# Fetching the first weight tile ahead of attention, taking weight signs from other words, and splitting the block loads between two queues

## Chip, cores and metric

The kernel runs on one core of one Trainium2 chip. The metric is the device time of one execution in microseconds. The change is judged by the median of several executions of the kernel before and after it.

## What is computed

A retention layer feeds two feed-forward layers. For each of 16 (batch, head) pairs, 768 steps:

```python
state = gamma * state + outer(k[t], v[t])
y[t]  = scale * (q[t] @ state)
x  = y laid out as (1536 tokens, 512)
x  = softplus(x @ w_in) @ w_out                        # m = 0, d_ff = 2048
h  = x @ w2_in
out = (h * clip(h + 3, 0, 6) / 6) @ w2_out              # m = 1
```

The four weight matrices come as 64-bit floats, and are made 32-bit floats on the chip.

## The kernel before

**Attention.** Tokens are taken in 12 units of 128 (two batches of six). Units 0 to 3 (`START`) run first, alone: k and q of a unit are loaded, turned on TensorE by transposes (`ident,k` and `ident,q`), copied out (`kT` by ScalarE, `qT` by VectorE), and give scores (`qT,kT`), masked by VectorE (`pw`), the product with the state (`qT,st`), the new state (`vs,k`) and the inner product (`pw,vs`). The result is split into `x_hi` (ScalarE) and `x_lo` (VectorE), the two parts of x that the GEMM uses. Units 4 to 7 run the same steps between the GEMM's blocks. Units 8 to 11 (`FIRST` and later) have no transposes on TensorE: `blocks` (L446) loads k and q in 16 small DMAs each, of 16 KB in pieces of 128 bytes, into tiles `kb` and `qb`, both halves of the buffer `raw_0`, and VectorE transposes them in 32x32 blocks into `cv` tiles (`in_blocks`). Both have one buffer, so a unit's loads wait until the unit before has been transposed.

**GEMM.** Each matrix is cut into 16 tiles of 256 KB (32-bit); tokens into three chunks of 512. A block of G1 is h = x @ w_in for one tile f (12 matmuls of 512 columns: hi x hi, hi x lo, lo x hi for four parts of the contraction), a block of G2 adds g @ w_out to four accumulating banks, two tiles later (`LAG`). Blocks alternate, G1 and G2, over m, chunk and f: 2304 matmuls of 512 columns, 192 blocks. At the end of a chunk the four accumulating banks are evacuated as the next `x_hi` and `x_lo`.

**Weights.** `weight` (L266) makes one tile: `fetch` (L283, SP, 512 KB of 64-bit words into `raw`), `bits` (ScalarE, the low word's top bits into `cv`), the sign, the high word scaled and clamped, `merge` (VectorE, shift and or), then the high part `w[:, 0]` (ScalarE, `high`) and the low part, either by VectorE (`low`) or by GpSimd as an accumulating DMA (`add`, L323). `sign` (L294) writes the top half of each `cv` word as a 16-bit float, reading the top 16 bits of the high word. For odd tiles of m = 0 and all of m = 1 (`SCALED`) ScalarE scales the high word (`scale`) and VectorE clamps it (`clamp`, one pass); for the others VectorE does both in two passes (`scaled`, `capped`). There are five raw buffers in the first stage, three later, and four `cv` buffers. Tiles of m = 0 are all made in the first pass over f, tiles of m = 1 while m = 0's last chunk and m = 1's first run.

**Order.** The order on each engine is set while the program is built. `Plan` (L25) holds tasks with an engine, a cost, a due time, what they follow and which buffers they take; `run` simulates the engines and emits tasks in the order in which that simulation starts them. Costs and due times so only set the order; on the chip each engine runs its queue in order and waits by semaphores. Every emitted operation has line 44 in the profile, and tiles tell them apart. DMAs are issued by SP (`nc.sync`), the accumulating ones by GpSimd (`nc.gpsimd`); a DMA on SP reuses one of eight semaphores and waits until the DMA eight before it has landed. The due time of the first tile's fetch is set on L329 (`begin + 15`, behind unit 0's and 1's loads).

```python
for e in range(2):                                            # blocks, L450
    r = slice((2 * g + e) * 32, (2 * g + e + 1) * 32)
    for p in range(NP):
        nc.sync.dma_start(out=tile_of(n)[r, p].rearrange("t (x d) -> t x d", x=4), in_=src[g, e, :, p])
```

```python
when -= EDGE * (u < START and eng in ("DVE", "ACT"))          # task, L429
```

Of the kernel before, what the change touches and what calls it, by code (L numbers as in the profile page):

```python
# [10 lines left out]
F32 = mybir.dt.float32  # L11
F32R = mybir.dt.float32r
U32 = mybir.dt.uint32
U16 = mybir.dt.uint16
F16 = mybir.dt.float16
AF = mybir.ActivationFunctionType
ALU = mybir.AluOpType
PSUM = bass.MemoryType.PSUM
P = 128
# [106 lines left out]

PSX, TT, TS, ACP, ACS = 0.61, 0.62, 0.36, 0.49, 0.55
GEMM = 2.73


@with_exitstack
def kernel(ctx, tc, q, k, v, w1_in, w1_out, w2_in, w2_out, table, out):
# [17 lines left out]
    MORE = 2  # L150
    AHEAD = 3
    HOLD = 8.0
    EDGE = 3.0

    def BY_DVE(n):
        return n < 6 or n < 2 * NF and n % 4 != 0

    def SCALED(n):
        return n >= 2 * NF or n % 2 == 1

    tc.nc.scalar.preload_act_table_set("softplus")

# [59 lines left out]
    half = fixed.tile([P, 1], F32, name="half")  # L222
    three = fixed.tile([P, 1], F32, name="three")
    nc.vector.memset(half, -0.5 + 7.5 * 2.0 ** -12)
    edge = fixed.tile([P, 1], F32, name="edge")
    nc.vector.memset(three, 3.0)
    nc.vector.memset(edge, 32767.5 * 2.0 ** -60)


    G = [(m, c, f) for m in range(2) for c in range(NC) for f in range(NF)]  # L230
# [35 lines left out]
    def weight(m, o, f, number):  # L266
        key = m, o, f
        made = conv[0] if m == 0 else []
        use = due[("G2" if o else "G1"), min(m * NC * NF + f, len(G) - LAG)] - 4.0

        def raw():
            return at_slot((f"raw{m}", key))

        def low_word():
            return raw()[:, :, 0]

        def y():
            return raw()[:, :, 1]

        def w():  # L280
            return at_slot((f"cv{m}", key))

        def fetch():  # L283
            src = words[m][o]
            if o:
                nc.sync.dma_start(out=raw().rearrange("p n t -> p (n t)"), in_=src[f * P:(f + 1) * P, :])
            else:
                nc.sync.dma_start(out=raw().rearrange("p (k n) t -> p k (n t)", k=KD),
                                  in_=src[:, 2 * f * P:2 * (f + 1) * P].rearrange("(k p) f -> p k f", p=P))

        def bits():
            nc.scalar.activation(w(), low_word(), AF.Relu, scale=2.0 ** -29 * (1 - 2.0 ** -12), bias=half)

        def sign():  # L294
            top = raw().bitcast(U16)[:, :, 3]
            to = w().bitcast(F16).rearrange("p (n x) -> p n x", x=2)[:, :, 1]
            nc.scalar.activation(to, top, AF.Identity, scale=-2.0 ** -60, bias=edge)

        def scale():
            nc.scalar.activation(y().bitcast(F32), y().bitcast(F32), AF.Copy, scale=2.0 ** -112)  # L300

        def clamp():
            nc.vector.tensor_scalar(y().bitcast(F32), y().bitcast(F32), -TOP, TOP, ALU.max, ALU.min)

        def scaled():
            nc.vector.tensor_scalar(y().bitcast(F32), y().bitcast(F32), 2.0 ** -112, -TOP, ALU.mult, ALU.max)

        def capped():
            nc.vector.tensor_scalar(y().bitcast(F32), y().bitcast(F32), TOP, None, ALU.min)

        def merge():
            nc.vector.scalar_tensor_tensor(w(), y(), 3, w(), ALU.logical_shift_left, ALU.bitwise_or)

        def high():
            nc.scalar.activation(w_part(key, 0), w().bitcast(F32), AF.Copy)

        def negative():
            nc.scalar.activation(w_part(key, 1), w().bitcast(F32), AF.Copy, scale=-1.0)

        def low():  # L320
            nc.vector.tensor_tensor(w_part(key, 1), w().bitcast(F32), w_part(key, 0).bitcast(F32), ALU.subtract)

        def add():  # L323
            nc.gpsimd.dma_start(out=w_part(key, 1).bitcast(F32), in_=w().bitcast(F32), accum_op=ALU.add)

        raw_k, cv_k = (f"raw{m}", key), (f"cv{m}", key)
        cv, part = [(f"cv{m}", cv_k)], [("w", ("w", key))]
        tail = 1.5 if BY_DVE(number) else 7.0
        T["F", key] = t0 = nc.add("SP", 0.45, fetch, due=begin + 15 if number < 1 else use - tail - 8.0, take=[(f"raw{m}", raw_k)], load=1.45 if o else 1.75)  # L329
        t1 = nc.add("ACT", 0.65, bits, [t0], use - tail - 3.5, take=cv)  # L330
        t2 = nc.add("ACT", 0.57, sign, [t1], use - tail - 2.9)
        if SCALED(number):
            t3 = nc.add("ACT", 0.57, scale, [t2], use - tail - 2.3)
            t4 = nc.add("DVE", TS, clamp, [t3], use - tail - 1.9)
        else:
            t3 = nc.add("DVE", TS, scaled, [t2], use - tail - 2.3)
            t4 = nc.add("DVE", TS, capped, [t3], use - tail - 1.9)
        t5 = nc.add("DVE", TT, merge, [t4, t2], use - tail - 1.3, give=[raw_k])
        if BY_DVE(number):
            a = nc.add("ACT", ACS, high, [t5], use - 1.5, take=part, give=[cv_k] + made)  # L340
            b = nc.add("DVE", TT, low, [a], use - 0.7, give=[cv_k] + made)
        else:
            n = nc.add("ACT", ACS, negative, [t5], use - tail, take=part)
            b = nc.add("POOL", 0.9, add, [n], use - tail + 1, give=[cv_k] + made, load=1.6)
            a = nc.add("ACT", ACS, high, [n], use - 2.5, give=[cv_k] + made)
        T["W", key] = [a, b]
# [42 lines left out]
        nc.tensor.transpose(idle[:, i % NP, :], ident, ident)  # L389

    arena = [("arena", j) for j in range(LATE)]

    part = [slice(j * HALF, (j + 1) * HALF) for j in range(2)]

# [26 lines left out]
    def attend(u):  # L421
# [6 lines left out]
        def task(eng, cost, fn, after, when, take=(), give=(), load=0.0, hold=0.0):  # L428
            when -= EDGE * (u < START and eng in ("DVE", "ACT"))  # L429
            return nc.add(eng, cost, fn, after, when, [(p, k) for p, k in take], list(give) + mine, load, hold)  # L430

        def tile_of(n):
            return at_slot((n, u))

        def own(n):
            return [(f"{n}{ph}", (n, u))]
# [9 lines left out]
        def blocks(n):  # L446
            def go():
                src = {"qb": q, "kb": k}[n][b, :, i * C:(i + 1) * C, :].rearrange("(p g) (x t) (e d) -> g e t p x d", g=2, x=4, e=2)
                for g in range(2):
                    for e in range(2):  # L450
                        r = slice((2 * g + e) * 32, (2 * g + e + 1) * 32)
                        for p in range(NP):
                            nc.sync.dma_start(out=tile_of(n)[r, p].rearrange("t (x d) -> t x d", x=4), in_=src[g, e, :, p])
            return go

        def load(n, when, parts=1):
# [5 lines left out]
            at = [d["S" if ph else "Tk"] - 9.0 + x / 2 for x in range(3)]  # L462
        ik, iv = load("k", at[0], 2 if u == 0 else 1), load("v", at[2])
        if ph:
            ikb, iqb = (task("SP", 7.2, blocks(n), [], d["S"] - 25.0, take=own(n), load=2.0, hold=HOLD + d["S"] - 30.0) for n in ("kb", "qb"))
        else:
            iq = load("q", at[1])
        if u == START - 1:
# [34 lines left out]
        if whole:  # L503
# [12 lines left out]
            def masked(g):  # L516
                return lambda: nc.vector.tensor_tensor(at_slot(("pw", u))[:, g], bank(sc[g]),
                                                       full.rearrange("p (n t) -> p n t", n=1).to_broadcast([P, NP, C]), ALU.mult)
# [264 lines left out]
```

## Time and profile before

| | |
|---|---|
| median of 3 runs | 594.3 us (594.19 to 595.33) |
| the profiled execution, its own time | 594.75 us |
| its span | 593.0 us |
| TensorE matmul busy | 580.7 us (98%) |
| ScalarE (ACT) busy | 338.9 us (57%) |
| VectorE (DVE) busy | 302.0 us (51%) |
| GpSimd (POOL) busy | 34.4 us (6%) |

PE is TensorE's matmuls and PEld its weight loads. A busy share is a mean over stages; what one engine's work costs is read from the waits of the engine that sets the end in that stage. Time lines give the start of an instruction, its length, and in brackets the idle time of its engine before it with what ended it. [...] The trace names a buffer after the tile that first had it, so unit 8 to 11's loads appear as `raw`, and their transposed blocks as `cv`.

### The profile page before, as it was taken

What the parts mean: (1) busy time and instruction counts of PE and PEld (TensorE: products, weight loads), DVE (VectorE), ACT (ScalarE), POOL (GpSimd) and SP (SyncE); (2) the same over time, 40 slices, a digit from 0 to 9 for tenths busy, and PEclk for the clock granted to TensorE, in tenths of its full rate; (3) what the DMA queues carried; (4) which work ended last, traced back from release to release, by engine and by line L of the source; (5) the groups of instructions that cost most, each with busy time, mean ns of one, the idle gap of its engine ahead of it and who ended that gap; (6) DMA issues with size and microseconds to landing.
All of it is one profiled execution on the core that took longest, in us unless ns stands there. A gap on an engine that the chain in (4) does not pass through costs nothing.

```text
span 593.0 us, 9082 instructions
## 1 busy us (share of the span) xinstructions
PE 580.7 (98%) x3607; PEld 474.1 (80%) x3607; DVE 302.0 (51%) x531; ACT 338.9 (57%) x552; POOL 34.4 (6%) x46
## 2 busy tenths in 40 slices
PE   8999999999999899999999999999999999999997
PEld 7777877788777688888888788878888888888886
DVE  5998998776556333554555654452412222422223
ACT  3599999974323133788999999962212222222220
POOL 0000010000000000011111122210000000000000
PEclk9999999999999899999999999999999999999999
DMA  9998587513323410156567678720100000100001
GB/s 199 247 269 218 168 209 224 142 19 65 65 33 65 114 38 0 31 131 159 148 147 184 161 198 212 180 50 1 72 0 1 0 1 0 72 0 1 1 1 71
DMA packets 80763, 57.76 MB, mean 97 GB/s; under 512 B 53712, under 2 KB 70352, under 8 KB 80720
## 3 DMA queue, kind: packets, MB, share of 16 engines
q1 hardware_dynamic: 75248, 47.21, 29.1%
q0 software_dynamic: 5472, 9.96, 9.9%
q8 instruction: 28, 0.46, 0.3%
q14 instruction: 15, 0.12, 0.1%
HBM read 44.05 MB, written 3.15 MB: 80 GB/s over the span
## 4 chain that ended last, share of the span: by engine, by line
PE 52%; issue 18%; ACT 18%; DVE 4%; POOL 3%; SPq 3%; DMA 2%; POOLq 0%; DVEq 0%; ACTq 0%
PE banks L44 52%; ACT cv L44 8%; ACT w L44 4%; POOL w L44 3%; SPq L44 3%; ACT raw L44 2%; ACT e L44 1%; ACT hi L44 1%; DVE cv L44 1%; ACT g L44 1%; DMA w<-cv 1%; DVE raw L44 1%; DMA raw<-in_v_dram 1%; DVE g L44 0%; DMA out_dram<-e 0%
## 5 line engine op out<-in xcount | busy, mean ns | idle before, releaser
L44 PE MATMUL banks<-x_hi,w 128*128 128x512 f32 x768 | 253.6, 392 | 0.8 <-ACT w L44 0.3
L44 PEld LDWEIGHTS banks<-x_hi,w 128*128 128x128 f32 x768 | 144.0, 188 | 33.0 <-DVE g L44 1.1
L44 PE MATMUL banks<-x_lo,w 128*128 128x512 f32 x384 | 149.1, 389 | 0.0
L44 PE MATMUL banks<-hi,w 128*128 128x512 f32 x384 | 128.7, 397 | 0.0
L44 PE MATMUL banks<-w,hi 128*128 128x512 f32 (+1 forms) x386 | 118.5, 389 | 1.1 <-DVE x_lo L44 1.1
L44 ACT ACTIVATE e<-banks,three 128x512 f32<-128x512 f32 x48 | 32.8, 684 | 114.5 <-PE banks L44 107.1
L44 DVE TENSOR_TENSOR lo<-g,hi 128x512 fp32r<-128x512 f32 x96 | 66.2, 690 | 53.7 <-ACT hi L44 53.7
L44 DVE SCALAR_TENSOR_TENSOR g<-e,banks 128x512 f32<-128x512 f32 x48 | 33.1, 689 | 113.7 <-ACT e L44 113.4
L44 PEld LDWEIGHTS banks<-hi,w 128*128 128x128 f32 x384 | 72.8, 190 | 16.4 <-ACT hi L44 0.8
L44 PEld LDWEIGHTS banks<-w,hi 128*128 128x128 f32 x386 | 72.2, 188 | 16.7 <-DVE x_lo L44 1.9
L44 ACT ACTIVATE hi<-g 128x512 fp32r<-128x512 f32 x96 | 60.1, 626 | 43.9 <-DVE g L44 41.3
L44 PEld LDWEIGHTS banks<-x_lo,w 128*128 128x128 f32 x384 | 72.1, 188 | 14.6
L44 PE MATMUL banks<-lo,w 128*128 128x512 f32 x192 | 75.9, 395 | 0.5 <-DVE lo L44 0.5
L44 PE MATMUL banks<-w,lo 128*128 128x512 f32 (+1 forms) x193 | 74.9, 388 | 0.0
L44 ACT ACTIVATE w<-cv 128x512 fp32r<-128x512 f32 x102 | 61.2, 622 | 3.8 <-DVE cv L44 3.5
L44 ACT ACTIVATE cv<-raw,edge 128x512 f16<-128x512 uint16 x64 | 55.9, 880 | 1.4
L44 ACT ACTIVATE g<-banks 128x512 f32<-128x512 f32 x48 | 28.1, 586 | 45.9 <-PE banks L44 45.8
L44 POOL DMA_DIRECT2D w<-cv x38 | 33.4, 878 | 358.0 <-ACT w L44 346.7
L44 DVE TENSOR_SCALAR raw<-raw 128x512 f32<-128x512 f32 x80 | 33.9, 427 | 37.4 <-ACT raw L44 33.1
L44 ACT ACTIVATE cv<-raw,half 128x512 uint32<-128x512 uint32 x64 | 48.1, 756 | 1.7 <-DMA raw<-in_moe_w_out_dram 1.1
L44 DVE SCALAR_TENSOR_TENSOR cv<-raw,cv 128x512 uint32<-128x512 uint32 x64 | 43.9, 689 | 1.3
L44 PEld LDWEIGHTS banks<-lo,w 128*128 128x128 f32 x192 | 36.4, 189 | 8.7 <-DVE lo L44 1.5
(59 smaller groups left out, 359.7 us busy)
## 6 DMA issues: line engine op xcount, KB each, us to landing
raw<-in_moe_w_in_dram SPq DMA_DIRECT2D x32, 512.0 KB, 4.1
raw<-in_moe_w_out_dram SPq DMA_DIRECT2D x32, 512.0 KB, 3.7
w<-cv POOLq DMA_DIRECT2D x38, 256.0 KB, 4.1
out_dram<-e SPq DMA_DIRECT2D x11, 256.0 KB, 2.0
q<-in_q_dram SPq DMA_DIRECT2D x8, 256.0 KB, 5.4
v<-in_v_dram SPq DMA_DIRECT2D x8, 256.0 KB, 5.9
k<-in_k_dram SPq DMA_DIRECT2D x7, 256.0 KB, 5.6
raw<-in_k_dram SPq DMA_DIRECT2D x64, 16.0 KB, 1.8
```

Source lines behind the costliest of these rows:

```text
L44: return self.plan.tc.keep_in_program_order(getattr(self.engine, op)(*args, **kwargs))
```

## The change

The fetch of the first tile gets a due time ahead of every attention load. `EDGE`, by which the due times of VectorE's and ScalarE's work for units 0 to 3 are brought forward, goes from 3 to 6. For m = 0 the high word is scaled and clamped by VectorE in two passes for every tile; the sign is written by ScalarE from 32-bit words, for odd tiles from the raw integer ahead of these passes, for even tiles from the clamped word behind them. For m = 1 the scale stays on ScalarE and the sign is taken out of it: VectorE puts it in by a second merge (`masked`, and with 0x80000000, or). Of the 16 small loads of a unit's k, four go to GpSimd, of q eight.

```diff
+SIGN = 0.75
...
-    EDGE = 3.0
+    EDGE = 6.0
...
-    def SCALED(n):
-        return n >= 2 * NF or n % 2 == 1
+    def DIRECT(n):
+        return n % 2 == 1
...
-    edge = fixed.tile([P, 1], F32, name="edge")
     nc.vector.memset(three, 3.0)
-    nc.vector.memset(edge, 32767.5 * 2.0 ** -60)
...
+        def to():
+            return w().bitcast(F16).rearrange("p (n x) -> p n x", x=2)[:, :, 1]
+
         def sign():
-            top = raw().bitcast(U16)[:, :, 3]
-            to = w().bitcast(F16).rearrange("p (n x) -> p n x", x=2)[:, :, 1]
-            nc.scalar.activation(to, top, AF.Identity, scale=-2.0 ** -60, bias=edge)
+            nc.scalar.activation(to(), y().bitcast(I32), AF.Copy, scale=2.0 ** -100)
+
+        def late_sign():
+            nc.scalar.activation(to(), y().bitcast(F32), AF.Copy)
+
+        def masked():
+            nc.vector.scalar_tensor_tensor(w(), y(), 0x80000000, w(), ALU.bitwise_and, ALU.bitwise_or)
...
-        T["F", key] = t0 = nc.add("SP", 0.45, fetch, due=begin + 15 if number < 1 else use - tail - 8.0, take=[(f"raw{m}", raw_k)], load=1.45 if o else 1.75)
+        T["F", key] = t0 = nc.add("SP", 0.45, fetch, due=begin - 2 if number < 1 else use - tail - 8.0, take=[(f"raw{m}", raw_k)], load=1.45 if o else 1.75)
         t1 = nc.add("ACT", 0.65, bits, [t0], use - tail - 3.5, take=cv)
-        t2 = nc.add("ACT", 0.57, sign, [t1], use - tail - 2.9)
-        if SCALED(number):
-            t3 = nc.add("ACT", 0.57, scale, [t2], use - tail - 2.3)
-            t4 = nc.add("DVE", TS, clamp, [t3], use - tail - 1.9)
+        if m:
+            t2 = nc.add("ACT", 0.57, scale, [t0], use - tail - 3.0)
+            t3 = nc.add("DVE", TS, clamp, [t2], use - tail - 2.5)
+            t4 = nc.add("DVE", TT, masked, [t3, t1], use - tail - 2.0)
         else:
-            t3 = nc.add("DVE", TS, scaled, [t2], use - tail - 2.3)
-            t4 = nc.add("DVE", TS, capped, [t3], use - tail - 1.9)
-        t5 = nc.add("DVE", TT, merge, [t4, t2], use - tail - 1.3, give=[raw_k])
+            t2 = nc.add("ACT", SIGN, sign, [t1], use - tail - 2.9) if DIRECT(number) else None
+            t3 = nc.add("DVE", TS, scaled, [t0, t2], use - tail - 2.7)
+            t3 = nc.add("DVE", TS, capped, [t3], use - tail - 2.3)
+            t4 = t2 or nc.add("ACT", SIGN, late_sign, [t1, t3], use - tail - 1.9)
+        t5 = nc.add("DVE", TT, merge, [t3, t4], use - tail - 1.3, give=[raw_k])
...
+    SHARE = {"kb": 2, "qb": 1}
...
-                            nc.sync.dma_start(out=tile_of(n)[r, p].rearrange("t (x d) -> t x d", x=4), in_=src[g, e, :, p])
+                            (nc.gpsimd if p > SHARE[n] else nc.sync).dma_start(out=tile_of(n)[r, p].rearrange("t (x d) -> t x d", x=4), in_=src[g, e, :, p])
...
-            ikb, iqb = (task("SP", 7.2, blocks(n), [], d["S"] - 25.0, take=own(n), load=2.0, hold=HOLD + d["S"] - 30.0) for n in ("kb", "qb"))
+            ikb, iqb = (task("SP", 0.48 * 4 * (SHARE[n] + 1), blocks(n), [], d["S"] - 25.0, take=own(n), load=2.0, hold=HOLD + d["S"] - 30.0) for n in ("kb", "qb"))
```

What the planner makes of it, at three places. In these rows a name is an engine's own list of operations, without times.

SP at the start, before: the tables, then attention's loads (`k_0`, `q_0`, `v_0` are unit 0's first, and unit 4's when they come again), and weight tiles in `raw`.

```order
L44 DMA small<-in_tables_dram 128x20
L44 DMA k_0_121<-in_k_dram 128x4x64 x2
...
L44 DMA v_1_125<-in_v_dram 128x8x64
L44 DMA raw_0_69<-in_moe_w_in_dram 128x4x256
L44 DMA k_2_123<-in_k_dram 128x8x64
...
L44 DMA k_0_121<-in_k_dram 128x8x64
L44 DMA q_0_118<-in_q_dram 128x8x64
L44 DMA v_0_124<-in_v_dram 128x8x64
L44 DMA raw_3_72<-in_moe_w_out_dram 128x1024
```

And SP at the start with the change:

```order
L44 DMA raw_0_69<-in_moe_w_in_dram 128x4x256
L44 DMA small<-in_tables_dram 128x20
L44 DMA k_0_119<-in_k_dram 128x4x64 x2
...
L44 DMA v_1_123<-in_v_dram 128x8x64
L44 DMA k_2_121<-in_k_dram 128x8x64
...
L44 DMA k_0_119<-in_k_dram 128x8x64
L44 DMA raw_3_72<-in_moe_w_out_dram 128x1024
L44 DMA q_0_116<-in_q_dram 128x8x64
L44 DMA v_0_122<-in_v_dram 128x8x64
```

The first tile has gone from the ninth place to the first, and a w_out tile now stands ahead of unit 4's q and v.

TensorE at units 1 and 2, before (`vs_1` is unit 1's, `k_2` and `q_2` unit 2's):

```order
L44 MATMUL banks<-vs_1_131,k_1_122 64x64 x8
L44 MATMUL banks<-ident,k_2_123 128x128 x4
L44 MATMUL banks<-pw_135,vs_1_131 64x128 x8
L44 MATMUL banks<-ident,q_2_120 128x128 x4
L44 MATMUL banks<-qT_0_128,kT_0_127 128x128 x8
```

And with the change:

```order
L44 MATMUL banks<-vs_1_129,k_1_120 64x64 x8
L44 MATMUL banks<-ident,k_2_121 128x128 x4
L44 MATMUL banks<-ident,q_2_118 128x128 x4
L44 MATMUL banks<-pw_133,vs_1_129 64x128 x8
L44 MATMUL banks<-qT_0_126,kT_0_125 128x128 x8
```

Unit 2's q is turned ahead of unit 1's inner product now, so that product stands between it and the scores that need it. Up to the first GEMM matmul that is all that moved on TensorE.

GpSimd with the change, from the last accumulating copy of m = 0 (`w_1311`) to the first of m = 1 (`w_78`); before, these two kinds of copies follow each other with nothing between:

```order
L44 DMA w_1311<-cv_1_75 128x512
L44 DMA raw_0_69<-in_k_dram 32x4x32 x4
L44 DMA raw_0_69<-in_q_dram 32x4x32 x8
L44 DMA raw_0_69<-in_k_dram 32x4x32 x4
L44 DMA raw_0_69<-in_q_dram 32x4x32 x8
L44 DMA raw_0_69<-in_k_dram 32x4x32 x4
L44 DMA raw_0_69<-in_q_dram 32x4x32 x8
L44 DMA raw_0_69<-in_k_dram 32x4x32 x4
L44 DMA raw_0_69<-in_q_dram 32x4x32 x8
L44 DMA w_78<-cv_0_74 128x512
```

Twelve loads of each of the units 8 to 11 have come to GpSimd, and all stand ahead of m = 1's copies. On TensorE the scores of units 8 to 11 moved with them: they stood behind 38, 42, 47 and 51 blocks of the GEMM, and stand behind 36, 39, 44 and 50.

## Rows read from the trace of the kernel before

**Rows 1.** The page, part 1: busy us, share of the span, instructions.
```profile
PE 580.7 (98%) x3607; PEld 474.1 (80%) x3607; DVE 302.0 (51%) x531; ACT 338.9 (57%) x552; POOL 34.4 (6%) x46
```

**Rows 2.** Windows: stretch, its length; busy us (instructions) by engine; clock; DMA share; GB/s.
```profile
core 0: us, PE busy (x) PEld busy (x) DVE busy (x) ACT busy (x) POOL busy (x), PEclk, DMA share, GB/s
27.11:113.56 86.45, 85.56 (x804) 67.55 (x805) 77.39 (x150) 84.28 (x141) 4.88 (x6) 1.00 0.78 213
...
200.00:320.00 120.00, 120.00 (x593) 98.78 (x592) 55.71 (x98) 85.15 (x139) 12.17 (x14) 0.99 0.41 102
320.00:392.00 72.00, 70.64 (x309) 57.45 (x309) 38.02 (x65) 69.71 (x117) 14.78 (x17) 1.00 0.72 174
```

**Rows 3.** Timeline of PE around unit 11's scores: start, length, operation [idle before].
```profile
194.41 0.62 PE L44 MATMUL banks<-x_hi,w 128*128 128x512 f32 x2
...
198.09 0.69 PE L44 MATMUL banks<-cv,cv 64*64 64x64 f32 x32 [2.61 <-DVE cv L44]
198.71 0.50 PE L44 MATMUL banks<-hi,w 128*128 128x512 f32 x1
...
203.25 0.69 PE L44 MATMUL banks<-cv,cv 64*64 64x64 f32 x32
```

**Rows 4.** Windows, the stretch behind that wait.
```profile
199.60:203.00 3.40, 3.40 (x10) 2.44 (x8) 1.83 (x3) 0.63 (x1) 0.00 (x0) 0.50 0.31 111
```

**Rows 5.** Timeline, ACT and PE at m = 1's first G2, PE at 387.
```profile
331.31 1.68 ACT L44 ACTIVATE w<-cv 128x512 fp32r<-128x512 f32 x3
...
333.45 0.60 ACT L44 ACTIVATE x_hi<-banks 128x512 fp32r<-128x512 f32 x1
...
334.95 0.74 PE L44 MATMUL banks<-w,hi 128*128 128x512 f32 x2 [1.13 <-DVE x_lo L44]
...
387.44 0.50 PE L44 MATMUL banks<-x_hi,w 128*128 128x512 f32 x1 [0.23 <-DVE g L44]
```

**Rows 6.** Timeline of PE, the first stage's waits.
```profile
45.29 0.50 PE L44 MATMUL banks<-lo,w 128*128 128x512 f32 x1 [0.23 <-DVE lo L44]
...
102.30 0.50 PE L44 MATMUL banks<-lo,w 128*128 128x512 f32 x1 [0.31 <-DVE lo L44]
...
113.56 0.50 PE L44 MATMUL banks<-x_hi,w 128*128 128x512 f32 x1 [0.32 <-ACT w L44]
```

**Rows 7.** Timeline of PE, the lead-in.
```profile
5.88 0.60 PE L44 MATMUL banks<-ident,q 128*128 128x128 f32 x4
...
17.24 1.16 PE L44 MATMUL banks<-qT,kT 64*128 64x128 f32 x16 [1.06 <-ACT w L44]
...
26.29 0.60 PE L44 MATMUL banks<-ident,q 128*128 128x128 f32 x4
...
27.11 2.11 PE L44 MATMUL banks<-x_hi,w 128*128 128x512 f32 x8 [0.21 <-ACT x_hi L44]
```

**Rows 8.** Timeline of SP, the first and the last of eight rows of block loads.
```profile
124.59 7.45 SPq L44 DMA_DIRECT2D raw<-in_k_dram  x16
...
186.46 8.54 SPq L44 DMA_DIRECT2D raw<-in_q_dram  x16
```

**Rows 9.** Groups by line and shape: count | busy us, mean ns of one | idle before.
```profile
L44 ACT ACTIVATE cv<-raw,edge 128x512 f16<-128x512 uint16 x64 | 55.9, 880 | 1.4
L44 DVE SCALAR_TENSOR_TENSOR cv<-raw,cv 128x512 uint32<-128x512 uint32 x64 | 43.9, 689 | 1.3
L44 DVE TENSOR_SCALAR raw<-raw 128x512 f32<-128x512 f32 x80 | 33.9, 427 | 37.4 <-ACT raw L44 33.1 <-ACT cv L44 3.4
L44 POOL DMA_DIRECT2D w<-cv x38 | 33.4, 878 | 358.0 <-ACT w L44 346.7 <-PE banks L44 7.7 <-DVE lo L44 3.3
L44 ACT ACTIVATE raw<-raw 128x512 f32<-128x512 f32 x48 | 31.9, 665 | 0.8
```

**Rows 10.** Windows, a stretch in which the DMA engines are full.
```profile
20.00:25.00 5.00, 5.00 (x78) 4.27 (x78) 4.40 (x10) 3.40 (x6) 0.00 (x0) 1.00 1.08 272
```

**Rows 11.** SP's timeline for q of units 0 and 4; each one's landing, by tile.
```profile
2.19 0.51 SPq L44 DMA_DIRECT2D q<-in_q_dram  x1
...
18.41 2.06 SPq L44 DMA_DIRECT2D q<-in_q_dram  x1
...
DMA to landing us min/median/max: 3.5/3.5/3.5
...
DMA to landing us min/median/max: 7.7/7.7/7.7
```

More of the change, by code (lines that the diff above doesn't have):

```diff
@@ L13 @@
 U32 = mybir.dt.uint32
-U16 = mybir.dt.uint16
+I32 = mybir.dt.int32
 F16 = mybir.dt.float16
```

## The prediction

> **What bounds the kernel now.** I read the page first: TensorE is busy for 580.7 of 593.0 us [rows 1], so nothing beside it can bring more than its 12 us of idle time and whatever time it works slowly. Then the windows by stage [rows 2]: in the first stage (27 to 114 us, where m = 0's 32 weight tiles are converted) ScalarE is busy for 84.28 of 86.45 us and VectorE for 77.39, yet TensorE for 85.56. In 320 to 392 us (m = 1's tiles) ScalarE has 69.71 of 72. The chain of waits would name ScalarE for all of that, but the gain there is only what TensorE waits, so I went through TensorE's timeline for its gaps. Back-to-back matmuls of 512 columns are drawn 0.39 us long and follow every 0.23 (two span 0.62, first of [rows 3]), so a gap costs 0.16 us more than the idle time drawn before it.
>
> The gaps that matter are these. (a) The block loads: the scores of unit 11 start at 198.09 after 2.61 us idle, for VectorE's `cv`, the transposed q blocks. [...] (b) At m = 1's first G2, 1.13 us for `x_lo`; SP and VectorE have nothing late there, but ScalarE evacuates that chunk's first bank at 333.45, behind a run of `w` copies from 331.31; and 0.23 us at 387.44 [rows 5]. (c) Three short waits in the first stage, 0.23, 0.31 and 0.32 us [rows 6]. (d) The lead-in: the first GEMM matmul starts at 27.11 [rows 7].
>
> **Block loads.** SP issues 16 loads in 7.45 us, 0.466 each, and is never idle between 124.59 and 195.00 (186.46 + 8.54) [rows 8]: 70.4 us for four units, 17.6 a unit. TensorE runs ahead of that at unit 11. The change leaves SP 12 + 8 loads, 20 x 0.466 = 9.3 us, and gives GpSimd 4 + 8. No row has such a load on GpSimd. Below, its price is SP's 0.466; the nearest row on its own engine is the accumulating copy, 0.878 us [rows 9], which also has 128 rows to describe; doubled, 1.76, is my upper end. I take 0.88: 12 x 0.88 = 10.5 us a unit, beside SP's 9.3 plus 1.1 for k and v. Both fit into 17.6, so the wait goes, and with it the slow stretch: 2.61 + 0.16 - 0.1 (usual hand-over) = 2.7, and 4.54 - 2.95 = 1.6. **Gain 4.3 us** (ends: 4.3 and, for 1.76, a loss, below). What is late next is unit 9: in the new order its scores stand only three GEMM blocks behind unit 8's (four before). Its k load can start when unit 8's k blocks are transposed, right behind the block of G1 17; from there to its scores TensorE has 5.6 blocks x 2.72 = 15.2 us and some 3 us of unit 8's own matmuls, 18. VectorE's two transposes and the product take 2.1 us, the landing about 2, other work of VectorE about 1: 13 us stay for 12 loads, so a price up to about 1.1 us is hidden.
>
> **Weight conversion.** m = 0: sixteen odd tiles lose ScalarE's scale (0.665) and gain a second VectorE tensor-scalar (0.427); all 32 keep a sign operation that reads 32-bit words and still writes 16-bit ones. Its price is not in the trace: between 0.665 (the scale, 32-bit input) and 0.880 (the present sign, same output) [rows 9]; I take 0.88, since the output is what sets it apart from the other rows. ScalarE falls by 16 x 0.665 = 10.6 us to 73.6 of 86.45, VectorE rises by 6.8 to 84.2. So VectorE becomes as full as ScalarE is now. The three waits of (c) cost 0.86 + 3 x 0.16 = 1.3 us; they end on ScalarE's side, and half of them may come back on VectorE's. **Gain 0.8** (ends: 1.3, and a loss of 2.2, one tile's chain of tensor-scalars, merge and low part, 2 x 0.427 + 2 x 0.689). m = 1: ScalarE loses 32 x 0.880 = 28 us, VectorE gains 32 merges of 0.689 = 22 us; in 200 to 392 us ScalarE falls from 154.9 to 127 and VectorE rises from 93.7 to 116 of 192 [rows 2], both with room, so the extra VectorE work costs nothing as long as that idle 76 us stands beside it. ScalarE then reaches the evacuation sooner: 1.13 + 0.23 + 2 x 0.16 = 1.7, **gain 1.5** (ends 1.7 and 0).
>
> **First tile ahead.** One 512 KB fetch goes before every attention load. At the 272 GB/s of 20 to 25 us [rows 10] it takes 524/272 = 1.9 us. q of unit 0 lands at 2.19 + 3.5 = 5.7 [rows 11] and TensorE takes it at 5.88 [rows 7], so attention starts late by between 0.4 (the issue alone) and 1.9 us; the queue is empty at first, so I take 1.1. Against that: the tile's fetch no longer stands between v of unit 1 and k of unit 2, its conversion leaves VectorE's way at 15 us, and in the new order q of unit 2 is transposed ahead of unit 1's last product, so that the 1.06 us wait for that q at 17.24 [rows 7] is covered by it. By the scores of unit 2 the delay is gone. Then SP's new order puts one w_out fetch (512 KB, 1.9 us) ahead of unit 4's q, which lands at 18.41 + 7.7 = 26.1 [rows 11] and is taken at 26.29, 0.8 before the first GEMM. All that lies before it in the queue is the same, only begun sooner by what the first fetch fills at the start. The GEMM so starts between 0.3 earlier and 1.9 later; I take **0.5 us lost**. The earlier due times (EDGE) only reorder, and are in this.
>
> **The sum.** -4.3 - 0.8 - 1.5 + 0.5 = -6.1 us. The profiled execution took 594.75 us, so 588.65; the median of the runs is 0.45 lower, so **588.2 us**.
>
> **Rivals.** *VectorE takes ScalarE's place in 27 to 114 us.* For it: 84.2 of 86.45 us busy. Against: its queue has fewer kinds of work that wait on TensorE. Price: the 0.8 isn't won and one chain of 2.2 is lost, 591.2. Chance 0.14.
>
> *Unit 9 waits a little.* At 1.3 us a load GpSimd is 12 x 0.2 = 2.4 us late: 590.6, or 592.2 if the clock falls again as at 199.6 (1.6 us). Chance 0.12.
>
> *Unit 9 waits long, and the kernel gets slower.* [...] From 1.6 us a load on, 12 x 0.5 = 6 us are late and the gain is gone; at 1.76 it is 7.9 + 1.6 for the clock: 588.2 + 9.5 = 597.7. Against it: 38 accumulating copies took 0.878 on the mean, beside a VectorE that in 320 to 392 us was busy half the time [rows 2, 9]. Chance 0.07. [...]
>
> *The lead-in pays in full.* Both fetches delay the GEMM by 1.9 us and one wait is added: 3 us lost in place of 0.5, 590.7. Against it: unit 2's covered wait. Chance 0.07.
>
> **How the numbers follow.** The forecast has 0.60; its own range is 586.3 to 590.3. Two in ten are left out beyond 585.8 (every gain at its upper end and the GEMM 0.3 earlier, 594.3 - 4.3 - 1.3 - 1.7 - 0.3 = 586.7, less 0.9 for short gaps that I didn't count) and 592.2, the short wait of unit 9 with the slow clock behind it. About 0.2%, 1.2 us, is what a measurement can tell from no change: 593.1 and less is faster. That takes in the forecast (0.60), nearly all of VectorE's case and the lead-in's (0.12 and 0.06) and most of unit 9's short wait (0.09): 0.87. The rest of these, 0.04, is the same; the long wait and the tail of the short one are slower, 0.09.
>
> **What would show it.** Right: no wait of unit 11's scores, the clock at its upper level throughout the middle, loads on GpSimd near 0.9 us, m = 1's first G2 without a wait for `x_lo`, the first GEMM matmul at 27.0 to 28.5 us, ScalarE's share in the first stage below VectorE's. Wrong: a wait of unit 9's scores for `cv`, loads of over 1.1 us on GpSimd, a row of waits for `w` with VectorE as the releaser between 30 and 110 us, or a granted clock of 0.50 in the lead-in.

## The result, and the profile after

The changed kernel took 587.17 us (median of 4 runs, 587.12 to 587.69), the kernel before 594.57 beside it: a ratio of 0.9876 (95% interval 0.9859 to 0.9893). On another chip, later, it took 587.21 (6 runs) against 593.53: 0.9908 (0.9886 to 0.9930). Its profiled execution took 587.69 us, 7.06 less than that of before. The forecast was 588.2, and 6.1 less.

TensorE's work is the same 3607 matmuls, so the 7 us must be found between them. The stages of [rows 2] and the stretch of [rows 4] in the windows of the changed kernel (columns as there):

```profile
27.11:113.56 86.45, 85.46 (x815) 68.50 (x812) 83.20 (x169) 78.13 (x131) 4.79 (x5) 1.00 0.76 214
200.00:320.00 120.00, 120.00 (x557) 99.17 (x557) 70.54 (x122) 79.79 (x137) 13.92 (x16) 1.00 0.46 115
320.00:392.00 72.00, 72.00 (x319) 59.61 (x318) 44.82 (x75) 52.96 (x92) 13.93 (x16) 1.00 0.64 154
199.60:203.00 3.40, 3.40 (x21) 2.77 (x17) 0.64 (x2) 0.18 (x1) 0.00 (x0) 1.00 0.52 156
```

In the first stage VectorE and ScalarE have changed places (83.20 and 78.13 us busy; 77.39 and 84.28 before), and TensorE is no busier for it. In 320 to 392 us ScalarE is down from 69.71 to 52.96 and TensorE has no idle time left. The granted clock (PEclk, a share of TensorE's full speed) is 1.00 in every one of these stretches, also where [rows 4] had 0.50. TensorE's timeline at unit 11's scores, which waited 2.61 us in [rows 3]:

```profile
192.01 0.39 PE L44 MATMUL banks<-hi,w 128*128 128x512 f32 x1
192.33 0.69 PE L44 MATMUL banks<-cv,cv 64*64 64x64 f32 x32
192.95 0.50 PE L44 MATMUL banks<-x_hi,w 128*128 128x512 f32 x1
```

No wait, and the next matmul follows after 0.62 us. At m = 1's first G2, ScalarE's and TensorE's timelines, to be held against [rows 5]:

```profile
325.50 0.67 ACT L44 ACTIVATE e<-banks,three 128x512 f32<-128x512 f32 x1
326.07 0.58 ACT L44 ACTIVATE x_hi<-banks 128x512 fp32r<-128x512 f32 x1
...
328.76 0.39 PE L44 MATMUL banks<-x_hi,w 128*128 128x512 f32 x1
328.99 0.62 PE L44 MATMUL banks<-w,hi 128*128 128x512 f32 x2
```

The copy of the first `x_hi` starts 2.7 us ahead of the last matmul that runs before G2; before, it started at 333.45, 0.02 behind that matmul's start. The groups, with the new prices (columns as in [rows 9]):

```profile
L44 ACT ACTIVATE cv<-raw 128x512 f16<-128x512 int32 x16 | 12.7, 796 | 0.3
L44 ACT ACTIVATE cv<-raw 128x512 f16<-128x512 f32 x16 | 12.1, 785 | 0.0
L44 DVE SCALAR_TENSOR_TENSOR cv<-raw,cv 128x512 uint32<-128x512 uint32 x96 | 65.6, 688 | 1.6
L44 DVE TENSOR_SCALAR raw<-raw 128x512 f32<-128x512 f32 x96 | 40.4, 428 | 10.8 <-ACT raw L44 8.3 <-ACT cv L44 1.8
L44 POOL DMA_DIRECT2D raw<-in_q_dram x32 | 18.2, 572 | 11.6 <-DVE cv L44 11.2
L44 POOL DMA_DIRECT2D raw<-in_k_dram x16 | 8.9, 560 | 19.0 <-DVE cv L44 12.8 <-DVE g L44 5.5 <-issue 0.4
```

A block load costs GpSimd 0.57 us (0.88 was taken, 0.466 is SP's), a sign from 32-bit words 0.79 (0.88 was taken).

**A ledger by blocks.** All kernels here run the same 192 GEMM blocks in the same order, so the start of block n (the first of its twelve 512-column matmuls, counted in TensorE's timeline from block 0; each trace has 2301 of the 2304) can be compared between traces. The table has that start for blocks 0 and 28, the time gained (-) or lost against the profile of before in blocks 28 to 60 (the block loads) and 98 to 122 (m = 1's tiles), and the sum at the last block. Between blocks 60 and 98 and behind 122 all traces agree to 0.02 us. The last column has the median of the runs and, in brackets, the profiled execution, to which the columns before it belong. The experiments' names are explained below.

| kernel | block 0 | block 28 | 28 to 60 | 98 to 122 | sum | median (profiled) |
|---|---|---|---|---|---|---|
| before | 27.11 | 122.31 | | | | 594.57 (594.75) |
| changed | 28.58 | 121.96 | -4.31 | -2.41 | -7.08 | 587.17 (587.69) |
| changed, again (e9) | 27.42 | 121.97 | -4.31 | -2.41 | -7.07 | 587.21 (587.72) |
| e1, loads on SP only | 28.43 | 121.44 | -3.43 | -2.41 | -6.72 | 588.41 (588.40) |
| e2, split only | 27.54 | 122.66 | -4.31 | -1.29 | -5.24 | 589.54 (589.53) |
| e3, first tile late | 27.15 | 123.35 | -4.31 | -2.41 | -5.68 | 587.61 (589.13) |
| e4, first tile only | 27.49 | 121.77 | +0.95 | -0.81 | -0.40 | 594.83 (594.38) |
| e5, m = 0 only | 26.83 | 121.17 | -4.31 | -1.29 | -6.74 | 589.97 (588.06) |
| e6, m = 1 only | 28.30 | 123.43 | +1.48 | -2.41 | +0.18 | 592.11 (594.96) |
| e7, all on GpSimd | 27.69 | 121.06 | +9.22 | -2.41 | +5.56 | 600.43 (600.43) |
| e8, tile 0's sign early | 26.67 | 121.90 | -4.31 | -2.41 | -7.13 | 587.84 (587.64) |
| e10, four tiles eased | 26.90 | 122.40 | -4.31 | -2.39 | -6.62 | 588.45 (588.17) |
| e11, m = 0 undone | 27.50 | 121.79 | -4.31 | -2.41 | -7.24 | 588.21 (587.54) |
| e12, m = 1 undone | 28.24 | 121.20 | -4.31 | -1.30 | -6.72 | 588.08 (588.05) |

So between these two profiles the change gained 0.36 us up to block 28, 4.31 at the block loads and 2.41 at m = 1. Three things limit what one row says. The kernel before ran beside e1 to e12 with medians of 593.42 to 593.95, and scattered there from 591.1 to 596.9. The profiles of e3 and e6 lie 1.5 and 2.9 us above their medians, that of e5 1.9 below.

The profile of before has the slow stretch of [rows 4], and not all its executions have one: of 62 beside the experiments, 26 have a mean granted clock of 0.994 to 0.997 (the profiled one has 0.996) and a median of 594.2 us, and 36 have 0.999 to 1.000 and a median of 592.9. Against these 36 the change gains 5.7 us, not 7.1.

And some kernels run the same operations in the same order on every engine until the block loads begin. The changed kernel, e1, e7, e9 and e12 do (e12 but for one memset), and start block 28 at 121.06 to 121.97, on the mean 121.5; before, e2 and e6 do, and start it at 122.31 to 123.43, on the mean 122.8; e4 and e11 do, at 121.8. So the first stage and the lead-in gained between 0.3 and 2.4 us, 1.3 by the means; 0.36 is the lower end.

### The profile page after: what moved, and what is told of

Read it like the earlier page. It is cut to its first block, busy times and chain, and to the rows that moved or that the text cites. A ratio compares the mean times of both kernels' runs of the same rounds, so it can differ in the third digit from the quotient of the medians.

```text
span 585.9 us, 9119 instructions
## 1 busy us (share of the span) xinstructions
PE 576.8 (98%) x3607; PEld 473.5 (81%) x3607; DVE 324.8 (55%) x578; ACT 303.2 (52%) x504; POOL 61.7 (11%) x94
## 4 chain that ended last, share of the span: by engine, by line
PE 94%; DVE 3%; DMA 1%; issue 0%; SPq 0%; DVEq 0%
PE banks L44 94%; DMA q<-in_q_dram 1%; DVE raw L44 1%; DVE cv L44 1%; DVE w L44 0%; DMA out_dram<-e 0%; DVE qT L44 0%; DVE pw L44 0%; SPq L44 0%; DVE st L44 0%; DVE e L44 0%; DVE g L44 0%; DVE vs L44 0%; DVE x_lo L44 0%; DVEq L788 0%
## 5 line engine op out<-in xcount | busy, mean ns | idle before, releaser
L44 PE MATMUL banks<-hi,w 128*128 128x512 f32 x384 | 126.8, 392 | 0.0
L44 DVE SCALAR_TENSOR_TENSOR cv<-raw,cv 128x512 uint32<-128x512 uint32 x96 | 65.6, 688 | 1.6
L44 ACT ACTIVATE g<-banks 128x512 f32<-128x512 f32 x48 | 28.6, 595 | 57.6 <-PE banks L44 57.3
L44 DVE TENSOR_SCALAR raw<-raw 128x512 f32<-128x512 f32 x96 | 40.4, 428 | 10.8 <-ACT raw L44 8.3
L44 PEld LDWEIGHTS banks<-w,lo 128*128 128x128 f32 x193 | 36.2, 188 | 7.5
```

The source lines that it names most:

```text
L44: return self.plan.tc.keep_in_program_order(getattr(self.engine, op)(*args, **kwargs))
```

## Experiments

### Is it the split that took the wait away? (e1, e2)

e1 is the changed kernel with the loads back on SP:

```diff
-                            (nc.gpsimd if p > SHARE[n] else nc.sync).dma_start(...)
+                            nc.sync.dma_start(...)
-            ... task("SP", 0.48 * 4 * (SHARE[n] + 1), blocks(n), ...
+            ... task("SP", 7.2, blocks(n), ...
```

> The changed kernel with all block loads on SP again (and the planner told so). Theory 1, the split between the queues took away the wait of unit 11 and the slow clock behind it: both come back, 587.2 + 4.3 = 591.5 us, with TensorE idle for 2 to 3 us before unit 11's scores and a granted clock of 0.50 behind it. Theory 2, the wait went because the weight conversion of m = 0 ends sooner and so the buffers come free sooner: the loads start at 120.1 in place of 124.6, their last one is issued at 120.1 + 70.4 = 190.5, unit 11's scores could start at 190.5 + 3.1 = 193.6 and stand at about 195.0 on TensorE, so nothing waits: 587.2 us, no idle time of TensorE over 0.3 us between 140 and 210.

588.41 us, ratio 0.9916 (0.9884 to 0.9948). That is neither theory's number, but nearer to theory 2's 587.2. SP's timeline, its first and last row of block loads, and TensorE's at unit 11:

```profile
119.56 7.45 SPq L44 DMA_DIRECT2D raw<-in_k_dram  x16
...
184.40 8.12 SPq L44 DMA_DIRECT2D raw<-in_q_dram  x16
```
```profile
195.41 0.69 PE L44 MATMUL banks<-cv,cv 64*64 64x64 f32 x32 [0.81 <-DVE cv L44]
196.04 0.50 PE L44 MATMUL banks<-hi,w 128*128 128x512 f32 x1
```

Without the split the loads begin 5.0 us sooner than in [rows 8] and end 2.5 sooner (192.52 for 195.00). The wait shrinks from 2.61 to 0.81 us, and the granted clock behind it is 1.00 (196 to 204 us). 3.43 of the 4.31 us are gained without the split.

e2 is the kernel before with the split and its planner cost added, the lines of the change on `SHARE` and nothing else.

> The kernel before with the block loads split as in the change, nothing else. Theory 1 and theory 2 both let the wait go: 594.6 - 4.3 = 590.3 us. A rival, that the earlier scores of unit 9 (three GEMM blocks behind unit 8's) need the earlier start of the loads too: unit 8's or 9's scores wait, by up to the 4.5 us by which the loads start later here, 590.3 to 594.8, with the granted clock at 0.50 behind a wait of over 2 us.

589.54 us, ratio 0.9935 (0.9908 to 0.9962), where 590.3 was expected, and the ledger has all 4.31 us at the block loads. Units 8 and 9 did not wait. So the split is enough for this wait, but most of the gain comes without it. Another 1.29 us came at m = 1, where this kernel's conversion is untouched.

### What the parts on the weights bring (e5, e6, e11, e12)

e5 and e6 give the kernel before the new conversion for one matrix pair alone:

```diff
         # e5: tiles of m = 0 as in the change, of m = 1 as before
+            t2 = nc.add("ACT", SIGN, sign, [t1], ...) if DIRECT(number) else None
+            t3 = nc.add("DVE", TS, scaled, [t0, t2], ...)
+            t3 = nc.add("DVE", TS, capped, [t3], ...)
+            t4 = t2 or nc.add("ACT", SIGN, late_sign, [t1, t3], ...)
         # e6: tiles of m = 1 as in the change, of m = 0 as before
+            t2 = nc.add("ACT", 0.57, scale, [t0], ...)
+            t3 = nc.add("DVE", TS, clamp, [t2], ...)
+            t4 = nc.add("DVE", TT, masked, [t3, t1], ...)
```

> The kernel before with the new conversion for m = 0's tiles alone (ScalarE's sign from 32-bit words, both passes over the high word on VectorE). Theory: it takes 1.8 us out of the first stage (the three waits and the hand-overs behind them), and it ends the conversion sooner, so the block loads start at about 120 and not at 124.6: of unit 11's wait 1.0 us is left, as with the loads on SP alone, and the slow clock is gone, 3.3 us more. 594.6 - 1.8 - 3.3 = 589.5 us. The rival, my prediction's term: 0.8 us in the first stage and no effect on the block loads, 593.8 us, with unit 11's wait at 2.6 us and the granted clock at 0.50 behind it.

589.97 us (588.06 to 592.19 in 10 runs), ratio 0.9934 (0.9911 to 0.9957), where 589.5 was expected and 593.8 by my prediction's term. Unit 11 doesn't wait at all in the profile, and the clock is 0.999 or 1.000 in all ten runs. Why, stands in the next rows. VectorE's merge of the last tile in `raw_0` and SP's first block load behind it, in the kernel before (VectorE's and SP's timelines):

```profile
123.84 0.69 DVE L44 SCALAR_TENSOR_TENSOR cv<-raw,cv 128x512 uint32<-128x512 uint32 x1
```

That merge ends at 124.53, and the first load is issued at 124.59 [rows 8]. The same in e5, with the last row of loads and unit 11's scores:

```profile
119.81 0.68 DVE L45 SCALAR_TENSOR_TENSOR cv<-raw,cv 128x512 uint32<-128x512 uint32 x1
```
```profile
120.52 7.45 SPq L45 DMA_DIRECT2D raw<-in_k_dram  x16
...
182.66 8.40 SPq L45 DMA_DIRECT2D raw<-in_q_dram  x16
```
```profile
194.26 0.69 PE L45 MATMUL banks<-cv,cv 64*64 64x64 f32 x32
```

The conversion ends 4 us sooner, the buffer comes free 4 us sooner, the last issue ends at 191.06 in place of 195.00, and the scores, some 3 us behind it (3.1 before, 2.9 in e1), are in time at 194.26.

An early start of the loads is not enough by itself: what counts is their end against the place that the scores have on TensorE. In e4 (below) the loads also run on SP alone and start at 121.98, 2.6 us sooner than before, but the planner put unit 11's scores one block further ahead (behind 50 blocks, 51 before and in e5), and they wait longer. TensorE's timeline in e4:

```profile
195.82 0.69 PE L44 MATMUL banks<-cv,cv 64*64 64x64 f32 x32 [3.61 <-DVE cv L44]
```

> The kernel before with the new conversion for m = 1's tiles alone. Theory: the 2.4 us that the changed kernel gains between blocks 98 and 122 come from this part, 592.2 us, and x_hi stands behind fewer w copies on ScalarE. Rival: half of them come from the moved scores and block loads (with the split alone 1.3 us were gained there), 593.3 us. Unit 11's wait and the slow clock behind it stay as before by both.

592.11 us, ratio 0.9979 (0.9956 to 1.0002): by the time alone no gain is shown, and theory and rival can't be told apart, since the kernel before took 593.86 beside it. The ledger has the theory's 2.41 us between blocks 98 and 122. In the profile the wait of unit 11 is there (3.06 us), and the granted clock is 0.50 behind it (199 to 203 us).

e11 and e12 take the same parts out of the changed kernel again (the old lines put back for m = 0, or for m = 1).

> The changed kernel without its part on m = 0's tiles (the old sign, odd tiles scaled by ScalarE). Theory: split and m = 0's conversion each take away unit 11's wait, so with the split that stays away though the block loads start at 124 to 126 again; what is lost is the first stage's 1.8 us: 589.0 us, ScalarE at 97% of the first stage. Rival: unit 8's and 9's scores, which the planner has put further ahead (behind 35 and 38 GEMM blocks), now come before their loads and wait 1 to 3 us: 590 to 592 us.

588.21 us, ratio 0.9918 (0.9899 to 0.9937), and in the profile no wait of units 8 to 11. Three of the six runs have a clock of 1.000 and took 587.30 to 587.54, as the changed kernel does, the profiled one among them; three have 0.996 and took 588.87 to 589.06, and no trace shows where. The surprise is block 28: it starts at 121.79, as early as in the changed kernel, though ScalarE is busy for nearly all of the stage again. Its windows, 27 to 114 us:

```profile
27.00:114.00 87.00, 85.39 (x810) 68.44 (x811) 79.66 (x155) 86.53 (x147) 5.56 (x6) 1.00 0.78 215
```

So with the early fetch m = 0's new conversion brings the first stage little: block 28 starts at 121.8 without it (e4 and e11, the same order), and at 121.5 on the mean with it, within a spread of 0.9.

> The changed kernel without its part on m = 1's tiles (the old sign on ScalarE, no second merge). Theory: moving the scores and the loads alone already brought 1.3 of the 2.4 us between blocks 98 and 122 (as with the split alone and with m = 0's conversion alone), so 1.1 us is lost there: 588.3 us. Rival: the whole 2.4 us belong to m = 1's conversion: 589.6 us.

588.08 us, ratio 0.9917 (0.9892 to 0.9942), near the theory's 588.3; the ledger has its 1.1 us, 1.30 being left of 2.41. ScalarE's and TensorE's timelines at m = 1's first G2:

```profile
326.59 0.67 ACT L45 ACTIVATE e<-banks,three 128x512 f32<-128x512 f32 x1
327.16 0.57 ACT L45 ACTIVATE x_hi<-banks 128x512 fp32r<-128x512 f32 x1
...
328.63 0.73 PE L45 MATMUL banks<-w,hi 128*128 128x512 f32 x2 [0.24 <-DVE x_lo L45]
```

With the old conversion but the new order ScalarE's queue is 0.9 us further on against TensorE: `x_hi` starts 1.65 us behind the start of block 98 (325.51), and before it started 2.52 behind it (333.45 and 330.93). Most of the wait of [rows 5] is gone already.

### The lead-in (e3, e4, e8, e9)

e3 is the changed kernel with the first fetch at its old place; e4 is the kernel before with the new place. The lines are e3's; e4 has the same two the other way round:

```diff
-        ... fetch, due=begin - 2 if number < 1 else ...
+        ... fetch, due=begin + 15 if number < 1 else ...
```

> The changed kernel with the first weight tile's fetch at its old due time (behind unit 0's and 1's loads), EDGE still 6. Theory A, that fetch costs the lead-in 1.5 us by delaying k and q of unit 0 by 2.3 us, of which the wait for unit 2's q gives back 1.2: the first GEMM matmul starts at 27.1 again or a little sooner, 587.2 - 1.5 = 585.7 us. Theory B, the lead-in got longer by the new order of VectorE's and ScalarE's work (EDGE) and by the fetch of w_out ahead of unit 4's q: the first GEMM matmul stays at 28.6, 587.2 us.

> The kernel before with the first weight tile's fetch ahead of attention, nothing else (EDGE 3). Theory A: the first GEMM matmul starts 1.4 us later, at 28.5, and the time is 594.6 + 1.4 = 596.0 us. Theory B: the first GEMM matmul at 27.1, 594.6 us. Unit 0's scores start at 9.7 by both.

e3: first GEMM matmul at 27.15, as theory A says, but 587.61 us (0.9904; 0.9870 to 0.9937), as theory B says. In the profile, the slowest of the four (589.13), what was gained was lost again in the first stage. TensorE's timeline:

```profile
55.57 0.73 PE L44 MATMUL banks<-x_hi,w 128*128 128x512 f32 x2 [2.21 <-DMA w<-cv]
```

A weight tile waits for GpSimd's accumulating copy. e4: 594.83 us, ratio 1.0015 (0.9995 to 1.0035), first GEMM matmul at 27.49, unit 0's scores at 9.12. Its time is 1.4 us over the kernel before beside it (593.42), theory A's difference, but not for theory A's reason: the first GEMM matmul is 1.0 sooner than A says, and block 28 is 0.5 sooner than before. The loss stands at the block loads (+0.95, the longer wait above), and nine of its ten runs have a clock of 0.994 to 0.997. So the changed kernel's 28.58 is not the price of the fetch alone.

e9 is the changed kernel once more, unaltered.

> The changed kernel again, beside the next two and the kernel before on one chip. Theory: of the 1.47 us by which its first GEMM matmul was late in its one profile, some 0.5 are that execution's own (its k of unit 0 landed 0.6 us later than in the two experiments with the same order): first GEMM matmul at 27.7 to 28.4, and the time within 0.3 us of 587.2. Rival: 28.6 belongs to the order, and comes again.

587.21 us, and the first GEMM matmul at 27.42, sooner than the theory has it; the rival's 28.6 did not come again. TensorE's timeline, first the changed kernel's profile from before, then this one:

```profile
6.96 0.44 PE L44 MATMUL banks<-ident,k 128*128 128x128 f32 x2 [0.56 <-DMA k<-in_k_dram]
8.10 0.66 PE L44 MATMUL banks<-ident,q 128*128 128x128 f32 x4 [0.71 <-DMA q<-in_q_dram]
9.71 1.16 PE L44 MATMUL banks<-qT,kT 64*128 64x128 f32 x16 [0.95 <-DVE qT L44]
...
28.20 0.63 PE L44 MATMUL banks<-ident,q 128*128 128x128 f32 x4 [0.37 <-DVE cv L44]
```
```profile
7.50 0.66 PE L44 MATMUL banks<-ident,q 128*128 128x128 f32 x4 [0.77 <-DMA q<-in_q_dram]
9.12 1.16 PE L44 MATMUL banks<-qT,kT 64*128 64x128 f32 x16 [0.95 <-DVE qT L44]
...
27.06 0.60 PE L44 MATMUL banks<-ident,q 128*128 128x128 f32 x4
27.42 1.86 PE L44 MATMUL banks<-x_hi,w 128*128 128x512 f32 x7
```

Unit 0's q came 0.6 us later in the first, and unit 4's q made TensorE wait there and not here (it landed at 28.06; the bracket names VectorE's `cv`, which e9's transposes don't wait for): 1.16 us of the lead-in are one execution's. By block 12 both are at 73.1 and stay together, for in e9 TensorE waits more on the way. The longest wait that only e9 has is for VectorE's `x_lo`:

```profile
64.66 0.65 PE L44 MATMUL banks<-ident,k 128*128 128x128 f32 x4 [0.40 <-DVE x_lo L44]
```

e8 takes tile 0's sign from the raw integer too, so that its merge can go ahead of unit 0's steps:

```diff
-        return n % 2 == 1
+        return n % 2 == 1 or n == 0
```

> The changed kernel with tile 0's sign taken early, from the raw integer, like an odd tile's. Theory: in the changed kernel tile 0's sign waits for the clamped word and stands on ScalarE behind unit 0's kT, so VectorE's merge and low part of tile 0 come between unit 0's and unit 1's steps and delay unit 1's scores by 0.6 us, and the w_out fetch makes unit 4's q late, 0.5 us: with the early sign the merge lies ahead of unit 0's qT, and the first GEMM block stands ahead of unit 4's q. First GEMM matmul at 27.0 to 27.6 in place of 28.6, 586.3 us. Rival: the lead-in is set by the landing of unit 0's q alone, first GEMM matmul at 28.3 to 28.6, 587.2 us.

First GEMM matmul at 26.67, better than the theory's 27.0, and block 28 at 121.90 all the same: 587.84 us, ratio 0.9900 (0.9863 to 0.9937). The 586.3 us that the theory made of it did not come: this lead-in doesn't reach the end of the first stage.

### GpSimd's price, and where unit 9 decides (e7)

The changed kernel with `nc.gpsimd.dma_start` for all 32 loads of a unit, the planner's costs left alone.

> The changed kernel with every block load on GpSimd, all else in its order. It measures GpSimd's price and the point from which unit 9 decides. At 0.57 us a load a unit takes 32 x 0.57 = 18.3 us and its scores come some 4 us after the last issue: unit 9's loads start at 138.1, so its scores at 160, where TensorE wants them at 155.5, 4.5 us late; units 10 and 11 again some 5 and 2 us, with the granted clock at 0.50 behind each: 587.2 + 12 + 3 x 1.6 = 604 us (599 to 608). If GpSimd's price rises where VectorE runs tensor-scalars, to 0.75 us, each unit is 6 us later: about 620 us.

600.43 us, ratio 1.0117 (1.0075 to 1.0158), within the 599 to 608 that were expected. GpSimd's timeline, a row of loads, TensorE's three longest waits, and the windows behind them (153 to 157 us behind the first, and so on):

```profile
158.06 9.17 POOL L44 DMA_DIRECT2D raw<-in_k_dram  x16
```
```profile
153.03 1.67 PE L44 MATMUL banks<-cv,st 64*64 64x64 f32 x32 [2.44 <-DVE st L44]
161.69 0.69 PE L44 MATMUL banks<-cv,cv 64*64 64x64 f32 x32 [3.00 <-DVE x_lo L44]
...
189.88 0.69 PE L44 MATMUL banks<-cv,cv 64*64 64x64 f32 x32 [3.33 <-DVE cv L44]
```
```profile
153.00:157.00 4.00, 3.97 (x38) 3.39 (x39) 2.05 (x4) 1.52 (x3) 3.82 (x8) 0.57 0.14 31
162.00:166.00 4.00, 4.00 (x88) 3.16 (x82) 1.95 (x4) 1.26 (x2) 3.83 (x8) 1.00 0.13 29
190.00:194.00 4.00, 4.00 (x71) 3.38 (x72) 2.47 (x6) 1.26 (x2) 3.83 (x8) 0.62 0.12 28
```

0.573 us a load, as in the changed kernel, though GpSimd is hardly idle here. Unit 9's scores start at 161.69, 160 had been worked out. But the first long wait is unit 8's, at its product with the state, though unit 8's loads had all landed, and the third is unit 10's, at its inner product. In VectorE's queue the transposes of unit 9's k come before the state that unit 8 waits for, and VectorE stood 5.86 us at them. VectorE's timeline:

```profile
151.63 0.71 DVE L44 STREAM_TRANSPOSE cv<-raw 128x512 f32<-128x512 f32 x1 [5.86 <-DMA raw<-in_k_dram]
152.57 0.93 DVE L44 TENSOR_TENSOR st<-st,banks 128x256 f32<-128x256 f32 x2
```

So late loads of one unit hold up the unit before it, which the prediction's step on unit 9 didn't have. Unit 11's scores don't wait. In all the loads on GpSimd cost 9.22 + 4.31 = 13.5 us against the split, where 17 had been worked out. With twelve loads a unit GpSimd needs 6.9 us and not 18.3, so a wait for GpSimd's loads is real but far off.

### A version that tries to be faster (e10)

e8, and four of m = 0's tiles scaled by ScalarE again:

```diff
+    def EASED(n):
+        return n % 8 == 3
...
+            if EASED(number):
+                t3 = nc.add("ACT", 0.57, scale, [t0, t2], use - tail - 2.7)
+                t3 = nc.add("DVE", TS, clamp, [t3], use - tail - 2.3)
```

> The changed kernel with tile 0's sign early, and four of m = 0's 32 tiles scaled by ScalarE again, clamped by VectorE in one pass. Theory: with the new conversion VectorE, 83.7 of 87 us busy, has taken ScalarE's place in the first stage, so that the earlier GEMM of the run with tile 0's sign early was lost again by block 28; four tensor-scalars less on VectorE (4 x 0.428 = 1.7 us) keep some of it: block 28 at 120.3 to 121.3 in place of 121.9, 586.2 us (585.5 to 586.8). Rival: the first stage is bound by the transfers (DMA share 0.76 in it), and block 28 stays at 121.9: 587.2 us.

A miss: 588.45 us (586.51 to 593.59 in 12 runs), ratio 0.9928 (0.9907 to 0.9949), where 586.2 was expected. Block 28 starts at 122.40, neither at 120.3 to 121.3 nor at the rival's 121.9. VectorE has room (80.44 of 87 us), but a tile waits for GpSimd's copy, as in e3. TensorE's timeline:

```profile
53.99 0.73 PE L44 MATMUL banks<-x_hi,w 128*128 128x512 f32 x2 [1.59 <-DMA w<-cv]
```

No version was faster than the changed kernel.

## Why the prediction was right, step by step

**Block loads, -4.3.** Measured 4.31 against the profile of before: the wait and the slow stretch, each as worked out. The slow stretch is the block from 198.71 to 203.25 [rows 3], 4.54 us at a clock of 0.50 from 199.6 to 203.0 [rows 4]; in the changed kernel twelve matmuls of the same kind took 2.81 us (195.81 to 198.62) at 1.00, where 2.95 was taken. Executions of before without the slow stretch have less to lose there. And the step took it for granted that only a shorter queue could end the wait. It did not ask what sets the start of the 70.4 us: the merge that frees `raw_0`. The earlier end of m = 0's conversion alone takes the wait away (e5), the split alone too (e2), and in the changed kernel each is the other's spare (e1 loses 0.9 us at that place, e11's profile nothing). The 4.3 were rightly counted once, but the step gave them to the split alone.

**GpSimd's price, 0.88.** 0.57, nearer to the lower end. Unit 9 had its 13 us for 6.9 us of loads. VectorE's work beside a load changes it little. In the traces of the changed kernel and of e7, of 27 block loads that overlap a tensor-scalar 10 took 0.61 to 0.77 us and the rest 0.55 to 0.57; of the other 149, which overlap other VectorE work or none, not one took over 0.60, and the median is 0.55. So a load loses at most some 0.2 us (0.77 against 0.55), and no trace shows by what.

**Weight conversion of m = 0, -0.8, and the lead-in, +0.5.** Together -0.3; measured -0.36 at block 28 in the changed kernel and in e9. That these agree with the forecast is luck: e7 and e12, the same order up to there, have -1.25 and -1.11, and the means of the orders differ by 1.3. Taken apart, e9 has +0.31 and -0.66, the first profile +1.47 and -1.83. The step on the lead-in was wrong in its parts: unit 0's scores came 1.7 to 2.3 us late (9.12 and 9.71 against 7.43), where I took 1.1 and put the end at 1.9. That unit 2's wait of 1.06 us disappears was right, and it saved the sum. The first GEMM matmul was to start at 27.0 to 28.5; it did at 28.58, just outside, and at 27.42. Of the three waits of (c), which the step put on ScalarE's side, [rows 6] names two for VectorE's `lo`; all three are gone. The step on ScalarE gave 73.6 us and VectorE 84.2; they have 78.1 and 83.2. VectorE did become the fuller one, as the first rival says, but no chain was lost by it. What I did not see is that the lead-in hardly matters: from 26.67 to 28.58 us at block 0, block 28 starts at 121.9 (e8, e9, changed). Which part brings the first stage its gain stays open. The early first tile alone has 121.77 (e4), m = 0's part alone 121.17 in e5's fastest run; but e3, which has m = 0's part and the old place of the first tile, has 123.35 in its slowest, and one order alone spreads over 0.9 to 1.1 us.

**m = 1, -1.5.** The term that was mis-sized: 2.41. I took the idle time of two waits and 0.16 for each. Between blocks 98 and 100 the first gave 1.62: the six matmuls right behind the wait come slowly too, taking 1.68 us from 334.95 to the seventh at 336.63, where the changed kernel's take 1.36 (328.99 to 330.35). Between blocks 116 and 122 it was 0.80 where I had counted one gap of 0.39. The conversion alone brings all 2.41 (e6). But 1.3 of it come without the conversion too, from a moved order, e2's or e5's, by which ScalarE reaches `x_hi` 0.9 us sooner; so taking the conversion out of the changed kernel loses only 1.1 (e12). The 22 us of merges on VectorE cost TensorE nothing, as said. Over 200 to 392 us ScalarE has 132.8 us, where 127 had been worked out, and VectorE 115.4, where it was 116.

**The sum.** -6.1 against -7.06 in the profiles, -7.4 and -6.3 by the medians of the two chips. The mechanisms at the block loads and at m = 1 came as forecast; that the sum is this near is partly luck, for the errors have opposite signs: m = 1 gained more than counted, and by the means the first stage did too, while more than half of the kernel before's executions lack the slow stretch and have that much less to lose.

## What to carry to other kernels

Several edits of one change can each remove the same wait; alone each looks as if the whole gain were its own, and the sum of such terms is too large unless each is also taken out of the finished kernel. For a wait on a transfer, ask what frees the buffer that lets it start as well as how long the queue takes: here one engine's merge, 70 us ahead, decided together with the place of the scores. And a lead-in read in one profile carries an execution's own microsecond; count GEMM blocks further on before believing it, and compare traces of kernels that are the same up to there: they show how much of a difference is one execution's.

## What was not expected of the hardware

**Idle time and the clock.** The granted clock fell behind TensorE's waits of 2.61 us (before: 0.50 from 199.6 to 203.0 us), 3.06 (e6: 0.50 from 199 to 203), 3.33 (e7: 0.62 on the mean from 190 to 194) and 3.61 (e4: 0.79 on the mean from 196 to 204), and also behind one of 2.44 us in e7 (0.57 on the mean from 153 to 157); behind one of 3.00 us in the same trace it was 1.00 (162 to 166), as behind 2.21 (e3, 56 to 60) and 0.81 (e1, 196 to 204). In these traces the length of the wait alone doesn't tell which. Executions of the kernel before differ by it, the medians by 1.3 us (594.2 and 592.9, above), near the 1.6 of the slow stretch.

**The first matmuls.** e6 has the order of the kernel before up to block 0 and its first loads landed no later (q of unit 0 at 5.71, before at 5.74), yet block 0 came 1.19 us later. TensorE's timeline in e6, to be held against [rows 7], where the same four transposes of q took 0.60 us from 5.88 on:

```profile
5.78 1.06 PE L45 MATMUL banks<-ident,k 128*128 128x128 f32 x4
6.63 1.05 PE L45 MATMUL banks<-ident,q 128*128 128x128 f32 x4
8.64 1.16 PE L45 MATMUL banks<-qT,kT 64*128 64x128 f32 x16 [0.95 <-DVE qT L45]
```

They ran at little over half the pace (1.05 us for 0.60), while the profile's clock column shows 1.00 for 4 to 8 us in both traces; unit 0's scores came 1.21 us later (8.64 for 7.43). With the column at 1.00 no row shows what slowed them.
